# Converting float64 weights in a fused attention, SoLU and mixture-of-experts kernel: the magnitude pass rebiases the exponent, three VectorE steps instead of four

## The chip, the cores and the metric

One core of a Trainium2 chip runs the whole program. The metric is device time of one execution in microseconds; the kernel before has a median of 421.72 us over three runs (421.53 to 422.84). The profile is of one further execution that took 421.23 us, with a span of 419.5 us from its first to its last recorded instruction; the 1.73 us between the two lie outside the span.

## The reference

The program is three layers in a row, all in float32 apart from three inputs that arrive as float64:

```python
x = attn(q, k, v)                       # local band plus an attention pooled by 4; rows of 512
h = x @ w_in                            # (1152, 512) @ (512, 1024); w_in is float64
sm = softmax(h); solu = h * sm
ln = (solu - mu) / sqrt(var + 1e-6) * g_ln
x = (ln @ w_out).astype(float32)        # (1152, 1024) @ (1024, 512); w_out is float64
e = argmax(x @ w_gate); y = gate * relu(x @ w1[e]) @ w2[e]     # 8 experts, capacity from an input
```

`w_in` and `w_out` are random float32 values times a Python-side float64 factor, so their words are true float64 numbers of ordinary size (magnitudes of about 0.1 and less). The kernel turns each into a float32 and splits that into a high part and a low part for TensorE.

## The kernel before, in words

Work is tiled by 128 rows. There are nine row tiles, i = 0 to 8. For each tile, `loc_scores`, `loc_T` and `loc_AV` compute the local attention, `finish` (line 466) adds the pooled part to give `x32` (line 472) and splits it into `xh` (ScalarE, 478) and `xl` (VectorE, 479). `gemm1(i)` (491) is 24 TensorE matmuls of 128x512 into the two PSUM banks `gp`, three products (xh·wh, xl·wh, xh·wl) for each of four row blocks of `w_in`. `row(i)` (512) takes the row maximum `nm` on VectorE (515), the exponent on ScalarE (518), and one VectorE product (522), which is the last reader of `gp`: the first matmul of `gemm1(i+1)` waits for it. `gemm2(i)` follows a tile later, and after tile 8 come the experts, whose weights (32 chunks of 1 MB) stream in by DMA.

The conversion is `conv_steps(c)` (173), for eight pieces: c = 0 to 3 are the four row blocks of `w_in`, 4 to 7 the four pairs of row blocks of `w_out`. A piece is 128 x 1024 float64 numbers in one of three 1 MB buffers `rawb` (`conv_load`, 161). Below, "conv c" is piece c, `mag{c}` and `cv{c}` are its two tiles of 128x1024 words, and its operations are, by line of the kernel before:

- 185, ScalarE: `mag` is the absolute value of the high words, read as float32.
- 186, VectorE TENSOR_SCALAR: the high words shifted left by 3 and masked.
- 189, VectorE SCALAR_TENSOR_TENSOR: sign and top exponent bit of the high words or-ed in.
- 192, VectorE SCALAR_TENSOR_TENSOR: the low words shifted right by 29 and or-ed in. It is the last VectorE reader of `rawb`.
- 195, VectorE SCALAR_TENSOR_TENSOR, the guard: `cv` times (`mag` >= a threshold), which makes numbers below float32's range zero.
- 202, ScalarE, twice for conv 4 to 7: times `g_sb`; 208, ScalarE: the high part; 209, GpSimd (POOL): the low part, cv minus high part.

The tiles `mag` and `cv` come from one group of four buffers (tag t4), which they share with `he` and `sq` of `row`.

TensorE and SyncE keep the order in which the code stands (`manual_schedule`). VectorE, ScalarE and GpSimd are ordered when the program is built, by a scheduler with its own idea of durations; each then runs its instructions strictly in that order. `PLAN` (1056) says where the conversions stand in the code: conv 0 and 1 in the pooled attention, conv 2 to 4 ahead of tile 0, conv 5 beside `loc_scores(1)`, the first two steps of conv 7 in `gemm1(0)`, conv 6 and the rest of conv 7 after it. A load into `rawb` for conv c+3 is issued once 192 of conv c and its 185 are done.

Of the kernel before, what the change touches and what calls it, by code (L numbers as in the profile page):

```python
# [14 lines left out]
U32 = mybir.dt.uint32  # L15
AF = mybir.ActivationFunctionType
ALU = mybir.AluOpType
# [10 lines left out]
def kernel(  # L28
# [14 lines left out]
    nc = tc.nc  # L43
# [106 lines left out]
        nc.vector.tensor_scalar(cap_s, cap_f, float(CS), None, ALU.min)  # L150


    THR = float(np.uint32(897 << 20).view(np.float32))
    win_h, win_l, wout_h, wout_l = {}, {}, {}, {}
    raw64 = {}

# [16 lines left out]
    def conv_steps(c):  # L173

        raw = raw64.pop(c)
        n = 1024
        hl = raw.bitcast(U32).rearrange("p (n two) -> p n two", two=2)
        hi_w, lo_w = hl[:, :, 1], hl[:, :, 0]
        hf = raw.rearrange("p (n two) -> p n two", two=2)[:, :, 1]
        mag = bp.tile([P, n], F32, tag="t4", name=f"mag{c}", bufs=NT4)  # L180
        a = bp.tile([P, n], F32, tag="t4", name=f"cv{c}", bufs=NT4)
        au = a.bitcast(U32)

        def shift():
            nc.scalar.activation(mag, hf, AF.Abs)
            nc.vector.tensor_scalar(au, hi_w, 3, 0x3FFFFFFF, ALU.logical_shift_left, ALU.bitwise_and)

        def top():
            nc.vector.scalar_tensor_tensor(au, hi_w, 0xC0000000, au, ALU.bitwise_and, ALU.bitwise_or)

        def low():
            nc.vector.scalar_tensor_tensor(au, lo_w, 29, au, ALU.logical_shift_right, ALU.bitwise_or)

        def split():
            nc.vector.scalar_tensor_tensor(a, mag, THR, a, ALU.is_ge, ALU.mult)
            if c < KD:
                ch, cl, cc, nm = win_h, win_l, c, "in"
            else:
                ch, cl, cc, nm = wout_h, wout_l, c - KD, "out"
                for j in range(2):  # L200
                    aj = a[:, j * 512:(j + 1) * 512]
                    nc.scalar.activation(aj, aj, AF.Copy, scale=g_sb[:, 2 * cc + j:2 * cc + j + 1])
            g, o = divmod(cc, 2)
            if o == 0:
                ch[g] = ring.tile([P, 2048], F32R, tag="wh", name=f"w{nm}h{g}")
                cl[g] = ring.tile([P, 2048], F32R, tag="wl", name=f"w{nm}l{g}")
            sl = slice(o * n, (o + 1) * n)
            nc.scalar.activation(ch[g][:, sl], a, AF.Copy)
            nc.gpsimd.tensor_tensor(cl[g][:, sl], a, ch[g][:, sl].bitcast(F32), ALU.subtract)

        return [shift, top, low, split]

    def conv(c):
# [1117 lines left out]
```

## Time and profile before

| | |
|---|---|
| median of three runs | 421.72 us (421.53 to 422.84) |
| the profiled execution | 421.23 us, span 419.5 us |
| TensorE matmul (PE) busy | 355.6 us, 85% of the span |
| VectorE (DVE) busy | 202.3 us, 48% |
| ScalarE (ACT) busy | 167.8 us, 40% |
| GpSimd (POOL) busy | 120.2 us, 29% |
| mean granted clock of TensorE | 0.936 of full speed |

A timeline row of the profile reads: start, duration, engine, line, operation, out<-in, partitions x elements, count, and in brackets how long the engine was idle before and what ended that. A duration can contain waiting inside the instruction (for an SBUF port, say), which then does not show in brackets. The granted clock is 1.00 for 2.4 GHz and 0.50 for 1.2 GHz. Busy shares over the whole span say little here, since the program has stages with different limits: attention and conversion up to about 95 us, nine tiles of two matrix products up to about 245 us, the experts to the end.

### The profile page before, as it was taken

To read this page: it belongs to the slowest core of one execution; us is meant where nothing else is said; L and a number is where in the kernel's file an instruction comes from. 1 tells how busy PE (TensorE), PEld (TensorE's weight loads), DVE (VectorE), ACT (ScalarE), POOL (GpSimd) and SP (SyncE) were. 2 spreads that over 40 slices of the span, in tenths; PEclk is the share of its full clock that TensorE was granted. 3 is DMA by queue.
4 is the path that set the end of the run, shared out by engine and by line. 5 is a ranking of instruction groups with operands and counts; after the bars stand their busy time and mean duration, and the time that the engine had idled before them with its cause. 6 is when DMAs were issued, how large, how long until landed. Compare 5 with 4: busy or idle time off the path is not lost. (4 is left out here: it accounts for less than half of the span.)

```text
span 419.5 us, 7278 instructions
## 1 busy us (share of the span) xinstructions
PE 355.6 (85%) x2718; PEld 307.0 (73%) x2719; DVE 202.3 (48%) x486; ACT 167.8 (40%) x432; POOL 120.2 (29%) x170
## 2 busy tenths in 40 slices
PE   3546638299999999999999979679998999999991
PEld 3435526187767687777878769679988999999990
DVE  0685999866374979989445541102111111120210
ACT  3557537686686565565435312111120111111110
POOL 6693725479903020340220111001020202020111
PEclk9986558779999999999999999998999999999997
DMA  8998537233099345127196119999999740010001
GB/s 219 247 156 173 202 124 224 79 98 99 1 361 279 94 135 173 75 80 225 41 297 254 40 54 311 387 385 392 405 389 345 240 145 29 3 43 2 29 23 41
DMA packets 43783, 72.38 MB, mean 173 GB/s; under 512 B 15238, under 2 KB 17542, under 8 KB 42960
## 3 DMA queue, kind: packets, MB, share of 16 engines
q1 hardware_dynamic: 40080, 60.30, 46.3%
q0 software_dynamic: 3648, 11.30, 7.5%
q8 instruction: 39, 0.64, 0.6%
q14 instruction: 16, 0.13, 0.1%
HBM read 57.91 MB, written 15.52 MB: 175 GB/s over the span
## 5 line engine op out<-in xcount | busy, mean ns | idle before, releaser
L1016 POOL DMA_INDIRECT out_dram<-yo,js x16 | 15.6, 974 | 136.5 <-ACT yo L1013 113.2
L916 DVE TENSOR_SCALAR h<-ap 128x512 f32<-128x512 f32 x16 | 11.1, 692 | 71.0 <-PE ap L910 71.0
L500 PE MATMUL gp<-winh,xh 128*128 128x512 f32 x72 | 30.8, 428 | 13.3 <-DVE he L522 8.4
L918 ACT ACTIVATE h<-xp 128x512 f32<-128x512 f32 x16 | 9.6, 597 | 80.6 <-PE xp L910 80.6
L500 PE MATMUL gp<-winh,xl 128*128 128x512 f32 x72 | 31.6, 439 | 2.5 <-DVE xl L479 2.5
L500 PE MATMUL gp<-winl,xh 128*128 128x512 f32 x72 | 31.7, 440 | 0.0
L936 PE MATMUL yp<-h,wr 128*128 128x136 f32 x256 | 30.3, 279 | 0.0
L936 PEld LDWEIGHTS yp<-h,wr 128*128 128x128 f32 x256 | 30.0, 190 | 0.0
L607 DVE SCALAR_TENSOR_TENSOR prod<-x,rawb 128x512 f32<-128x512 f32 x40 | 28.3, 709 | 1.0 <-ACT x L568 0.6
L942 DVE COPY yT<-yp 128x512 f32<-128x512 f32 x7 | 4.8, 692 | 48.4 <-PE yp L936 42.0
L562 PE MATMUL xp<-wouth,lh 128*128 128x512 f32 x64 | 27.7, 433 | 0.0
L500 PEld LDWEIGHTS gp<-winh,xh 128*128 128x128 f32 x72 | 14.5, 202 | 16.1 <-issue 8.7
L562 PE MATMUL xp<-woutl,lh 128*128 128x512 f32 x64 | 26.2, 409 | 0.0
L670 POOL DMA_INDIRECT xd<-x,sloti x9 | 9.3, 1032 | 46.9 <-DVE efs L636 17.7
L415 ACT ACTIVATE e<-ls,lnm 128x70 f32<-128x70 f32 x68 | 20.6, 321 | 5.0 <-DVE lnm L412 4.9
L910 PE MATMUL xp<-xc,wr 128*128 128x136 f32 (+1 forms) x128 | 19.6, 307 | 1.6 <-DMA xg<-xd 1.6
L910 PEld LDWEIGHTS xp<-xc,wr 128*128 128x128 f32 x128 | 18.5, 196 | 1.8 <-issue 1.8
L500 PEld LDWEIGHTS gp<-winh,xl 128*128 128x128 f32 x72 | 14.4, 200 | 6.4 <-DVE xl L479 3.3
L910 PE MATMUL ap<-xc,wr 128*128 128x136 f32 (+1 forms) x128 | 19.0, 302 | 0.0
L936 PE MATMUL yp<-h,cpw 128*128 128x136 f32 (+1 forms) x128 | 19.0, 309 | 0.0
L936 PEld LDWEIGHTS yp<-h,cpw 128*128 128x128 f32 x128 | 18.7, 190 | 0.0
L562 PE MATMUL xp<-wouth,ll 128*128 128x512 f32 x64 | 18.6, 407 | 0.0
(262 smaller groups left out, 871.1 us busy)
## 6 DMA issues: line engine op xcount, KB each, us to landing
wr<-in_moe_w_dram SPq DMA_DIRECT2D x32, 512.0 KB
rawb<-in_moe_w_dram SPq DMA_DIRECT2D x16, 512.0 KB
cpw<-in_moe_w_dram SPq DMA_DIRECT2D x16, 512.0 KB
xd<-init POOLq DMA_DIRECT2D x2, 2056.0 KB, 17.4
xg<-xd SPq DMA_DIRECT2D x16, 257.0 KB
rawb<-in_moe_w_in_dram SPq DMA_DIRECT2D x8, 512.0 KB
rawb<-in_moe_w_out_dram SPq DMA_DIRECT2D x4, 1024.0 KB
xr<-x SPq DMA_DIRECT2D x9, 257.0 KB
```

What stands on the lines that cost most here:

```text
L415: nc.scalar.activation(e[:, a, pair], pv[:, pair], AF.Exp, bias=nm[:, u:u + 1], accum_out=sums[:, u:u + 1])
L500: nc.tensor.matmul(st["hp"][:, f * 512:(f + 1) * 512], xx[:, c * P:(c + 1) * P], ww[:, o * 1024 + f * 512:o * 1024 + (f + 1) * 512], start ...
L562: nc.tensor.matmul(st["ps"], xx[:, o * P:(o + 1) * P], ww[:, o * 512:(o + 1) * 512], start=(n == 0), stop=(n == 3 * KF - 1))
L607: nc.vector.scalar_tensor_tensor(prod, x2_t[i][:, :DM], 1.0, row, ALU.mult, ALU.mult, accum_out=st["lg"][:, e:e + 1])
L670: nc.gpsimd.indirect_dma_start(out=xd, out_offset=bass.IndirectOffsetOnAxis(ap=sloti, axis=0), in_=x2_t[i], in_offset=None, bounds_check=E ...
L910: nc.tensor.matmul(bank[:, j, :T], w[:, o:o + P], xc[:, c, :T], start=(c == 0), stop=(c == KD - 1))
L916: nc.vector.tensor_scalar(h, bank, 0.0, None, ALU.max)
L918: nc.scalar.activation(h, bank, AF.Relu)
L936: nc.tensor.matmul(bank[:, j, :T], w_t["w2", e, f // 4][:, o:o + P], h_t[e][f // 2][:, f % 2, :T], start=(f == 0), stop=(f == KF2 - 1))
L942: nc.vector.tensor_copy(yT, bank)
L1016: ins = nc.gpsimd.indirect_dma_start(out=out, out_offset=bass.IndirectOffsetOnAxis(ap=is_t[e][:, a:a + 1], axis=0), in_=yo_t.pop((e, a)), ...
```

## The change

[...] The first VectorE step takes the low words alone; the second shifts `mag` left by 3 and or-s it in; the third adds the sign bit. The guard (195) is gone. So there are three VectorE steps for each of eight conversions instead of four, and the second step now reads what ScalarE wrote, which the fourth did before.

```diff
-    THR = float(np.uint32(897 << 20).view(np.float32))
+    REBIAS = 2.0 ** -112
...
         def shift():
-            nc.scalar.activation(mag, hf, AF.Abs)
-            nc.vector.tensor_scalar(au, hi_w, 3, 0x3FFFFFFF, ALU.logical_shift_left, ALU.bitwise_and)
+            nc.scalar.activation(mag, hf, AF.Abs, scale=REBIAS)
+            nc.vector.tensor_scalar(au, lo_w, 29, None, ALU.logical_shift_right)
 
         def top():
-            nc.vector.scalar_tensor_tensor(au, hi_w, 0xC0000000, au, ALU.bitwise_and, ALU.bitwise_or)
+            nc.vector.scalar_tensor_tensor(au, mag.bitcast(U32), 3, au, ALU.logical_shift_left, ALU.bitwise_or)
 
         def low():
-            nc.vector.scalar_tensor_tensor(au, lo_w, 29, au, ALU.logical_shift_right, ALU.bitwise_or)
+            nc.vector.scalar_tensor_tensor(au, hi_w, 0x80000000, au, ALU.bitwise_and, ALU.bitwise_or)
 
         def split():
-            nc.vector.scalar_tensor_tensor(a, mag, THR, a, ALU.is_ge, ALU.mult)
             if c < KD:
```

The scheduler also puts the remaining instructions in another order. TensorE's order is the same in both. Lines from 195 on have a number lower by one in the changed kernel (472 becomes 471, 515 becomes 514). In the rows, a name ends with the piece or tile and a buffer number: `cv4_529` is conv 4's `cv`, `x32_0` is tile 0's.

VectorE, from conv 3 to the low part of tile 0's input, before:

```order
L186 TENSOR_SCALAR cv3_519<-rawb0_64 128x1024
L189 SCALAR_TENSOR_TENSOR cv3_519<-rawb0_64,cv3_519 128x1024
L192 SCALAR_TENSOR_TENSOR cv3_519<-rawb0_64,cv3_519 128x1024
L195 SCALAR_TENSOR_TENSOR cv3_519<-mag3_518,cv3_519 128x1024
L186 TENSOR_SCALAR cv4_529<-rawb1_65 128x1024
L189 SCALAR_TENSOR_TENSOR cv4_529<-rawb1_65,cv4_529 128x1024
L472 TENSOR_TENSOR x32_0_500<-ap_99,outd_115 128x512
L192 SCALAR_TENSOR_TENSOR cv4_529<-rawb1_65,cv4_529 128x1024
L412 TENSOR_REDUCE lnm1_557<-ls10_558 128x4
L479 TENSOR_TENSOR xl0_503<-x32_0_500,xh0_502 128x512
```

The same place in the changed kernel:

```order
L186 TENSOR_SCALAR cv3_516<-rawb0_64 128x1024
L189 SCALAR_TENSOR_TENSOR cv3_516<-mag3_515,cv3_516 128x1024
L192 SCALAR_TENSOR_TENSOR cv3_516<-rawb0_64,cv3_516 128x1024
L186 TENSOR_SCALAR cv4_525<-rawb1_65 128x1024
L189 SCALAR_TENSOR_TENSOR cv4_525<-mag4_524,cv4_525 128x1024
L192 SCALAR_TENSOR_TENSOR cv4_525<-rawb1_65,cv4_525 128x1024
L471 TENSOR_TENSOR x32_0_498<-ap_99,outd_115 128x512
L186 TENSOR_SCALAR cv5_587<-rawb2_66 128x1024
L411 TENSOR_REDUCE lnm1_552<-ls10_553 128x4
L189 SCALAR_TENSOR_TENSOR cv5_587<-mag5_586,cv5_587 128x1024
L411 TENSOR_REDUCE lnm1_552<-ls11_568 128x4
L478 TENSOR_TENSOR xl0_501<-x32_0_498,xh0_500 128x512
```

The guard of conv 3 is gone, the last step of conv 4 stands ahead of tile 0's `x32` where it stood behind it, and two steps of conv 5 with two row maxima stand between `x32` and `xl`.

VectorE, from the lsum of tile 1's local attention to the row maximum of tile 0, before:

```order
L418 TENSOR_SCALAR lsum1_556<-lsum1_556 128x8
L195 SCALAR_TENSOR_TENSOR cv5_592<-mag5_591,cv5_592 128x1024
L148 SCALAR_TENSOR_TENSOR cap_f_81<-capf2_549 128x1
L419 RECIPROCAL lsum1_556<-lsum1_556 128x8
L186 TENSOR_SCALAR cv7_642<-rawb1_65 128x1024
L150 TENSOR_SCALAR cap_s_82<-cap_f_81 128x1
L189 SCALAR_TENSOR_TENSOR cv7_642<-rawb1_65,cv7_642 128x1024
L192 SCALAR_TENSOR_TENSOR cv7_642<-rawb1_65,cv7_642 128x1024
L195 SCALAR_TENSOR_TENSOR cv7_642<-mag7_641,cv7_642 128x1024
L472 TENSOR_TENSOR x32_1_663<-ap_99,outd_115 128x512
L515 TENSOR_REDUCE nm0_671<-gp_108 128x1
```

The same place in the changed kernel:

```order
L417 TENSOR_SCALAR lsum1_551<-lsum1_551 128x8
L148 SCALAR_TENSOR_TENSOR cap_f_81<-capf2_544 128x1
L418 RECIPROCAL lsum1_551<-lsum1_551 128x8
L150 TENSOR_SCALAR cap_s_82<-cap_f_81 128x1
L189 SCALAR_TENSOR_TENSOR cv7_636<-mag7_635,cv7_636 128x1024
L192 SCALAR_TENSOR_TENSOR cv7_636<-rawb1_65,cv7_636 128x1024
L471 TENSOR_TENSOR x32_1_657<-ap_99,outd_115 128x512
L514 TENSOR_REDUCE nm0_665<-gp_108 128x1
```

Both guards are gone, and the first step of conv 7 stands further ahead: two steps of conv 7 are left between the lsum's reciprocal and `x32_1`.

ScalarE, from the high part of conv 5 to the exponent of tile 0, before:

```order
L208 ACTIVATE wouth0_537<-cv5_592 128x1024
L442 ACTIVATE eT10_630<-lt10_625 70x512
L442 ACTIVATE eT11_638<-lt11_633 70x512
L202 ACTIVATE cv7_642<-cv7_642,g_sb_78 128x512 x2
L478 ACTIVATE xh1_665<-x32_1_663 128x512
L208 ACTIVATE wouth1_697<-cv7_642 128x1024
L518 ACTIVATE he0_673,se0_674<-gp_108,nm0_671 128x1024
```

The same place in the changed kernel:

```order
L207 ACTIVATE wouth0_532<-cv5_587 128x1024
L201 ACTIVATE cv7_636<-cv7_636,g_sb_78 128x512 x2
L207 ACTIVATE wouth1_690<-cv7_636 128x1024
L441 ACTIVATE eT10_624<-lt10_619 70x512
L441 ACTIVATE eT11_632<-lt11_627 70x512
L477 ACTIVATE xh1_659<-x32_1_657 128x512
L517 ACTIVATE he0_667,se0_668<-gp_108,nm0_665 128x1024
```

The three passes for conv 7 stand ahead of the two copies `eT1` that tile 1's local attention needs on TensorE; they stood behind them, one of them just ahead of tile 0's exponent.

## Rows read from the trace of the kernel before

**Rows 1.** Stretches by engine: us, busy of PE, PEld, DVE, ACT, POOL; PEclk, DMA

```profile
59.00:83.00 24.00, 11.74 (x98) 8.38 (x98) 22.53 (x29) 15.03 (x45) 10.94 (x5) 0.78 0.48 143
...
95.00:240.00 145.00, 144.18 (x1119) 110.38 (x1118) 100.68 (x334) 84.95 (x243) 42.58 (x64) 1.00 0.48 156
...
262.00:323.00 61.00, 52.63 (x422) 51.67 (x421) 9.50 (x15) 8.32 (x14) 4.89 (x10) 0.97 1.05 389
```

**Rows 2.** TensorE's second longest wait after 83.1 us: us in total, times, longest

```profile
PE xp L910 <- issue: 3.0, 2, 1.6
```

**Rows 3.** TensorE's timeline from tile 0's first product to tile 1's

```profile
61.71 0.80 PE L500 MATMUL gp<-winh,xl 128*128 128x512 f32 x1 [2.19 <-DVE xl L479]
...
69.53 0.63 PE L438 MATMUL lt<-ident,e 128*70 128x128 f32 x4 [1.73 <-POOL e L421]
...
72.64 0.39 PE L500 MATMUL gp<-winl,xh 128*128 128x512 f32 x1
...
83.04 0.77 PE L500 MATMUL gp<-winh,xh 128*128 128x512 f32 x1 [8.38 <-DVE he L522]
```

**Rows 4.** VectorE's timeline, conv 2 to tile 0's xl

```profile
38.43 0.69 DVE L186 TENSOR_SCALAR cv<-rawb 128x1024 uint32<-128x1024 uint32 x1 [3.21 <-DMA rawb<-in_moe_w_in_dram]
...
46.81 2.73 DVE L186 TENSOR_SCALAR cv<-rawb 128x1024 uint32<-128x1024 uint32 x1
...
56.19 1.23 DVE L189 SCALAR_TENSOR_TENSOR cv<-rawb,cv 128x1024 uint32<-128x1024 uint32 x1
57.33 0.68 DVE L472 TENSOR_TENSOR x<-ap,outd 128x512 f32<-128x512 f32 x1
57.93 2.77 DVE L192 SCALAR_TENSOR_TENSOR cv<-rawb,cv 128x1024 uint32<-128x1024 uint32 x1
...
60.62 0.44 DVE L412 TENSOR_REDUCE lnm<-ls 128x4 f32<-128x280 f32 x1
60.98 0.68 DVE L479 TENSOR_TENSOR xl<-x,xh 128x512 fp32r<-128x512 f32 x1
```

**Rows 5.** VectorE's timeline, tile 1's lsum, conv 7's guard and tile 0's row

```profile
66.47 0.16 DVE L418 TENSOR_SCALAR lsum<-lsum 128x8 f32<-128x8 f32 x1
...
73.99 3.18 DVE L195 SCALAR_TENSOR_TENSOR cv<-mag,cv 128x1024 f32<-128x1024 f32 x1
...
77.69 1.21 DVE L515 TENSOR_REDUCE nm<-gp 128x1 f32<-128x1024 f32 x1
...
81.60 1.28 DVE L522 SCALAR_TENSOR_TENSOR he<-gp,se,he 128x1024 f32<-128x1024 f32 x1
```

**Rows 6.** GpSimd's timeline, conv 3's and conv 7's low part and tile 1's e

```profile
56.59 3.02 POOL L209 TENSOR_TENSOR winl<-cv,winh 128x1024 fp32r<-128x1024 f32 x1 [4.85 <-ACT winh L208]
68.11 1.37 POOL L421 TENSOR_TENSOR e<-e,lsum 128x560 f32<-128x560 f32 x1 [8.49 <-DVE lsum L419]
...
80.08 2.34 POOL L209 TENSOR_TENSOR woutl<-cv,wouth 128x1024 fp32r<-128x1024 f32 x1 [3.99 <-ACT wouth L208]
```

**Rows 7.** ScalarE's timeline around tile 0's row

```profile
70.20 1.26 ACT L442 ACTIVATE eT<-lt 70x512 f32<-70x512 f32 x2
77.20 1.33 ACT L202 ACTIVATE cv<-cv,g_sb 128x512 f32<-128x512 f32 x2 [5.74 <-DVE cv L195]
...
78.96 1.04 ACT L208 ACTIVATE wouth<-cv 128x1024 fp32r<-128x1024 f32 x1
79.91 1.09 ACT L518 ACTIVATE he<-gp,nm 128x1024 f32<-128x1024 f32 x1
```

**Rows 8.** TensorE alone in three stretches: us, busy; granted clock, DMA

```profile
83.00:89.00 6.00, 5.96 (x20) 0.50 0.14 39
```

**Rows 9.** All engines around a gap among the experts, as Rows 1

```profile
280.30:282.60 2.30, 0.00 (x0) 0.00 (x0) 0.00 (x0) 0.60 (x1) 0.00 (x0) 1.00 1.03 380
282.90:287.00 4.10, 4.10 (x24) 4.10 (x24) 0.69 (x1) 0.00 (x0) 0.00 (x0) 0.61 1.05 386
```

**Rows 10.** SyncE's timeline: the experts' first streamed chunks

```profile
254.43 16.73 SPq L707 DMA_DIRECT2D wr<-in_moe_w_dram  x16
```

## The prediction

> **What bounds the kernel now.** I read the table of stretches first. From 95 to 240 us TensorE is busy 144.2 of 145 us at a granted clock of 1.00 [rows 1]: nothing can be won there, but nothing is loose there either, so whatever starts earlier goes on earlier. From 59 to 83 us it is the other way round: TensorE is busy 11.7 of 24 us, VectorE 22.5 [rows 1]. So VectorE's queue bounds the program there, and that is where four of the eight conversions stand. Then TensorE's waits: after 83 us its longest is for 8.4 us [rows 3] and the next group sums to 3.0 us [rows 2]. The 8.4 us end with the first matmul of `gemm1(1)` at 83.04, which waits for VectorE's 522 of tile 0, the last reader of `gp` [rows 3].
>
> Why is 522 late? The last matmul of `gemm1(0)` starts at 72.64 and takes 0.39, so `gp` is whole at 73.03 [rows 3]. VectorE takes its row maximum `nm` only at 77.69, since the guard of conv 7 runs until 77.17 and `x32_1` follows it [rows 5]. Then `nm` is done at 78.90, but ScalarE's exponent starts at 79.91, because 208 of conv 7 stands ahead of it (78.96, 1.04 us) [rows 5, 7]. From the exponent's start to 83.04 it is 3.13 us.
>
> A second thing is to be seen in the durations. 192 of conv 4 takes 2.77 us at 57.93, where a three-operand step on 1024 words takes 1.23 [rows 4]; it ends at 60.70, one step after GpSimd's 209 of conv 3, which ends at 59.61 [rows 6]. 472 at 57.33 runs in the middle of that 209 and takes its usual 0.68 [rows 4, 6]. So the conversion steps, which read SBUF, do not run beside 209, while 472, which takes its products from PSUM, does; and each 209 (2.34 us alone [rows 6]) can cost the step that meets it up to that. The guard's 3.18 us at 73.99 and 186's 2.73 us at 46.81 are such cases, 186 alone taking 0.69 [rows 4, 5].
>
> **The change, part by part.** Eight guards of 1.2 us go, about 10 us of VectorE's time. The other three steps are of the same kind and size: one TENSOR_SCALAR (0.69), two SCALAR_TENSOR_TENSOR (1.23 each) [rows 4], and the scale in ScalarE's pass is an operand that the instruction has anyway; I count both at nothing. Where the trace has no such form (one operation in place of two, a contiguous operand in place of a strided one) the bounds are a step like 186, half as long, and one like 189: 0.5 us either way per step. What matters is the path, in four terms. I go from 38.43, where VectorE stops waiting for conv 2's data [rows 4]; that load was issued ahead of all this, so this point stays.
>
> *1. To `x32_0` (57.33).* From 38.43 on VectorE runs 13 conversion steps ahead of `x32_0`; now it is 11, since the guards of conv 1, 2 and 3 go and 192 of conv 4 comes in front of `x32_0`. That is 2 x 1.2 = 2.4 us less. But that 192 is the step that met 209 of conv 3, and its extra 1.55 us (2.77 less 1.22) now lie ahead of `x32_0`. Sum: 0.85 us earlier, at 56.5. Bounds: 2.4 earlier, if 209 is missed, and 0 with a whole 209 of 2.34.
>
> *2. From `x32_0` to `xl0`.* Before, 3.65 us (57.33 to 60.98) [rows 4]. Now 472 (0.6 from start to start), 186 of conv 5 (0.6), two row maxima (0.36 each from start to start) and 189 (1.2) stand there [rows 4]: 3.1 us, so `xl0` could start at 59.6. ScalarE, though, now has conv 4's two products by `g` (1.33), then `xh` (0.6, as `xl`), then 208 (1.04) [rows 4, 7] from 56.5 on, so 209 of conv 4 can start at about 59.5 and hold until 61.8. `xl0` reads SBUF alone, as the conversion steps do, so I take it that it waits: 61.8, and the first xl matmul, 0.73 us later as before (60.98 to 61.71), at 62.5 instead of 61.71: **0.8 us lost**. If `xl0` comes first, it is 60.3: 1.4 us won. This hangs on a tenth of a microsecond, so both ends are in the range.
>
> The Trainium skill's page SBUF — State Buffer (Who interferes with whom) says that the port pair of VectorE and GpSimd is an exclusive lock, taken by a VectorE instruction with two SBUF inputs or in a two-port mode, and that issue order decides who blocks. The trace agrees: 192 waited, 472, which reads PSUM, did not. By that rule alone `xl0`, with two SBUF inputs, waits out whatever is left of 209, 2.2 us as I took it; without it the sum would be 2.2 us better.
>
> *3. `gemm1(0)`.* Before, TensorE works for 6.1 us from 61.71, then waits 1.73 us for tile 1's `e` (421) until 69.53 [rows 3]; `e` waited for the lsum that stood behind guards [rows 5, 6]. Now it gets to that place at 68.6. After `xl0` (to 62.4) VectorE has 192 of conv 5 (to 63.6), 186 of conv 7 (64.2), six small ones of about 0.1 us, as 418 [rows 5], (64.8), and 189 of conv 7 (66.0); `e` follows within 1.4 us [rows 6], by 67.3, so this wait goes. 192 of conv 7 then ends at 68.5. ScalarE now does conv 7's products and high part (1.33 + 1.04) ahead of the copies `eT1` (1.26) [rows 7], so these end at 72.1 instead of 71.46. The last matmul ended 1.57 us after them (73.03), so `gp` is whole at 73.7: **0.6 us later than before**, the gain given back to the new order of ScalarE.
>
> *4. Tile 0's row.* Now nothing but `x32_1` (0.6) stands between the last products and `nm`: `nm` at about 73.8, done at 75.0, and nothing stands ahead of the exponent: 75.1 instead of 79.91. **4.8 us won**, and with 3.13 us as before `gemm1(1)` starts at 78.2 instead of 83.04.
>
> *5. The clock.* TensorE's idle time ahead of `gemm1(1)` shrinks from 8.4 to about 3 us. After the 8.4 us it works at clock 0.50, 1.2 GHz, from 83.0 to 89.0 [rows 8], which costs half, 3.0 us. After an idle stretch of 2.3 us among the experts it was at 0.61 on average over 4.1 us [rows 9], 1.6 us lost there, and some 2 with the edges. Between these I take 2.1 lost: **0.9 won**. Bounds: 0, as before, and 3.0, if it stays at 1.00.
>
> From there nothing else should move: TensorE has no gaps until 240 us, and the tiles' loads and stores follow its progress. Conv 6 loses its guard too, which nobody waits for. The experts' weights come at 389 GB/s with the DMA engines full from 262 to 323 us [rows 1], but their stream is issued from 254.43 on, behind the end of the last tile [rows 10], so it moves along. Sum: 4.8 + 0.9 = 5.7 us. Against the profiled execution, 421.23, that is 415.5. The median of the runs is 0.49 above it, so I predict 416.0.
>
> **The rivals.** A measurement here can tell about 0.3%, 1.3 us.
>
> *A. Luck with the port and the clock.* `xl0` gets ahead of 209, which brings the chain of term 3 forward by up to 2.2 us, and the clock keeps its level through the shorter gap (2.1 more): 416.0 less 4.3 is 411.7. For it: both hang on tenths of a microsecond. Against it: a gap of 2.3 us was enough to bring the clock down [rows 9], though the two that sum to 3.0 us [rows 2] left the stretch around them at 0.97 [rows 1].
>
> *B. The port takes the gain.* VectorE's remaining steps are closer together, so more of them can meet a 209. Each that conv 7's steps meet moves `eT1` by 2.34: one gives 418.3, two 420.7. For it: conv 7's guard met one in the trace [rows 5], and its steps now come sooner after 209 of conv 4. Against it: that one would have to be still running 5 us after its start, or conv 5's to start before 68.5.
>
> *C. ScalarE's new order makes it slower.* TensorE now waits for `eT1` behind conv 7's three ScalarE passes. The change is worth nothing from the point where `eT1` ends 4.8 us later than forecast, at 76.9, with the clock as low as before. With three 209 met (7.0 us) `gp` is whole at 80.7, and the clock's 0.9 goes: 415.5 + 7.0 + 0.9 is 423.4, and 423.9 as a median. Against it: only the 209 of conv 4 and of conv 5 are left for conv 7's steps to meet.
>
> *D. The gain is swallowed later.* Were the experts' stream not moved, TensorE, idle 8.4 us among them from 262 to 323 [rows 1], would wait that much more: 421.7. Against it: rows 10.
>
> **How the numbers follow.** The forecast, 414.0 to 418.0 with its own bounds (terms 1 and 5), has 0.6; A 0.12; B 0.15, most of it with one 209; C 0.05; D 0.08. The range reaches from 412.5, inside A, to 419.8, between B's two: outside lie the rest of A, the second step of B, C and D. Faster by over 0.3% (under 420.4): the forecast, A and most of B, 0.86. Within 0.3%: D and the end of B, 0.09. Slower: C, 0.05.
>
> **What would show it.** Right: the eight guards gone and nothing else longer; `nm` of tile 0 within 0.5 us of `x32_1`'s end and that right behind the last matmul's partners; the exponent right behind `nm`; TensorE's wait before `gemm1(1)` near 3 us in place of 8.4; the same order and length of everything after it. Wrong in a step: `x32_0` after 58, `xl0` before 60.5 or after 63, `eT1` ending after 74, a granted clock of 0.50 for 6 us after 78. Wrong as a whole: `gemm1(1)` earlier by 5 us and the end not.

## The result

| | before | after |
|---|---|---|
| median of four runs each, on one chip | 421.97 us (421.53 to 422.84) | 416.0 us (415.32 to 418.32) |
| the profiled execution, its span | 421.23 us, 419.5 us | 415.32 us, 413.6 us |
| VectorE busy | 202.3 us | 192.9 us |
| ratio to before, 95% interval | | 0.9866, 0.9824 to 0.9907 |

The kernel is 1.3% faster: 6 us, where 5.7 were predicted.

The scale 2**-112 in ScalarE's magnitude pass moves the exponent from float64's bias to float32's: the high word, read as float32, has the top eight of the eleven exponent bits, and 112 is (1023 - 127) / 8. What becomes of numbers below float32's range without the guard, no run here shows; there are none in this input.

VectorE's timeline in the kernel after, from conv 2's data to tile 0's row:

```profile
39.58 0.69 DVE L186 TENSOR_SCALAR cv<-rawb 128x1024 uint32<-128x1024 uint32 x1 [4.73 <-DMA rawb<-in_moe_w_in_dram]
...
47.68 3.26 DVE L192 SCALAR_TENSOR_TENSOR cv<-rawb,cv 128x1024 uint32<-128x1024 uint32 x1
50.86 2.84 DVE L186 TENSOR_SCALAR cv<-rawb 128x1024 uint32<-128x1024 uint32 x1
53.80 3.18 DVE L189 SCALAR_TENSOR_TENSOR cv<-mag,cv 128x1024 uint32<-128x1024 uint32 x1
...
58.16 0.68 DVE L471 TENSOR_TENSOR x<-ap,outd 128x512 f32<-128x512 f32 x1
...
61.22 2.84 DVE L478 TENSOR_TENSOR xl<-x,xh 128x512 fp32r<-128x512 f32 x1
...
73.70 0.69 DVE L471 TENSOR_TENSOR x<-ap,outd 128x512 f32<-128x512 f32 x1 [4.21 <-PE ap L458]
74.36 1.22 DVE L514 TENSOR_REDUCE nm<-gp 128x1 f32<-128x1024 f32 x1
```

These answer to [rows 4, 5]. No guard is left; `nm` stands directly behind `x32_1`, and VectorE, which was busy without a gap there, has waited 4.21 us for TensorE. Three steps in a row take about 3 us each (47.68 to 56.98), and `xl0` takes 2.84 in place of 0.68. GpSimd's timeline says why:

```profile
46.63 9.27 POOL L208 TENSOR_TENSOR winl<-cv,winh 128x1024 fp32r<-128x1024 f32 x3 [2.00 <-ACT winh L207]
61.16 2.34 POOL L208 TENSOR_TENSOR woutl<-cv,wouth 128x1024 fp32r<-128x1024 f32 x1 [5.26 <-ACT wouth L207]
```

The low parts of conv 1 to 3 now follow each other without a pause from 46.63 to 55.90, and each holds one step of VectorE; that of conv 4 starts 0.06 us before `xl0`. TensorE's timeline, for [rows 3], and then stretches of 1 us, for [rows 8] (columns as in [rows 1]; behind the busy times of the five engines stands the granted clock):

```profile
64.11 0.80 PE L499 MATMUL gp<-winh,xl 128*128 128x512 f32 x1 [3.12 <-DVE xl L478]
...
73.92 0.40 PE L499 MATMUL gp<-winl,xh 128*128 128x512 f32 x1
...
78.82 0.65 PE L499 MATMUL gp<-winh,xh 128*128 128x512 f32 x1 [2.86 <-DVE he L521]
```

```profile
79.00:80.00 1.00, 1.00 (x3) 0.81 (x3) 0.65 (x3) 1.00 (x3) 0.11 (x1) 0.50 0.00 0
...
81.00:82.00 1.00, 1.00 (x5) 0.77 (x4) 0.15 (x1) 1.00 (x3) 0.63 (x2) 0.50 0.07 16
82.00:83.00 1.00, 1.00 (x9) 0.85 (x7) 0.44 (x1) 1.00 (x3) 1.00 (x3) 0.82 0.00 0
```

The wait ahead of `gemm1(1)` is 2.86 us in place of 8.38, and TensorE works at a granted clock of 0.50 (1.2 GHz) for some 3.5 us after it, not 6.

**Where the time went.** One point that the prediction held fixed is not: conv 2's data landed at 38.43 before and at 39.58 now, and between 39.2 and 40.8 in the twelve traces that follow. SyncE issues that load at 22.04 before and at 22.99 now, but in the other traces (22.8 to 24.4) a later issue doesn't mean a later landing, and what moves it stays open. So times up to the end of `gemm1(1)` are counted from that landing in this document. The landing is the start of VectorE's step that waits for the DMA; `gp` is whole at the end of its last matmul; "rest" is the span less the end of `gemm1(1)`.

| us from the landing | landing | `x32_0` | first xl matmul | `gp` whole | `gemm1(1)` starts | ends | rest |
|---|---|---|---|---|---|---|---|
| before | 38.43 | 18.90 | 23.28 | 34.60 | 44.61 | 56.72 | 324.4 |
| after | 39.58 | 18.58 | 24.53 | 34.74 | 39.24 | 50.93 | 323.1 |

The span fell by 5.9 us: 1.15 were lost by the later landing, 5.37 won up to the start of `gemm1(1)`, 0.42 within it, and 1.26 in the rest.

### The profile page after: what moved, and what is told of

Same layout as the page of the kernel before. It is cut to its first block, busy times and chain, and to the rows that moved or that the text cites. A ratio compares the mean times of both kernels' runs of the same rounds, so it can differ in the third digit from the quotient of the medians.

```text
span 413.6 us, 7274 instructions
## 1 busy us (share of the span) xinstructions
PE 357.8 (86%) x2718; PEld 307.5 (74%) x2719; DVE 192.9 (47%) x478; ACT 167.6 (41%) x432; POOL 119.0 (29%) x170
## 5 line engine op out<-in xcount | busy, mean ns | idle before, releaser
L1015 POOL DMA_INDIRECT out_dram<-yo,js x16 | 15.6, 974 | 135.0 <-ACT yo L1012 111.7
```

What stands on the lines that cost most here:

```text
L1015: ins = nc.gpsimd.indirect_dma_start(out=out, out_offset=bass.IndirectOffsetOnAxis(ap=is_t[e][:, a:a + 1], axis=0), in_=yo_t.pop((e, a)), ...
```

## The experiments

All but one (the guard taken out of the kernel before) stand on the kernel after, and each has a profile; lines added by an edit shift the numbers behind them. Ratios are to the kernel before in runs of the same group; single runs of one kernel differ by 1% and more, so the fronts are read from the traces, in the measure above. Four of the traces ("fourth step, not 5, 7", "low part later", "warm early", "plan and warm") are of the longest run of their kernel, which bears on their column "rest":

| | landing | `x32_0` | first xl | `gp` whole | `gemm1(1)` | ends | rest | ratio, 95% interval |
|---|---|---|---|---|---|---|---|---|
| after again | 39.67 | 18.58 | 24.52 | 34.73 | 39.23 | 50.94 | 323.4 | 0.9857, 0.9806 to 0.9908 |
| fourth step, all | 39.23 | 17.85 | 23.97 | 35.43 | 45.09 | 56.28 | 323.9 | 1.0008, 0.9977 to 1.0038 |
| fourth step, conv 7 | 40.77 | 18.58 | 24.51 | 37.34 | 42.39 | 53.82 | 321.9 | 0.9922, 0.9889 to 0.9955 |
| fourth step, not 5, 7 | 40.52 | 17.85 | 23.97 | 38.36 | 43.45 | 55.21 | 325.4 | 0.9914, 0.9876 to 0.9952 |
| before, no guard | 39.46 | 20.84 | 25.47 | 36.63 | 41.13 | 53.73 | 324.0 | 0.9919, 0.9878 to 0.9959 |
| warm | 40.56 | 18.59 | 24.53 | 34.74 | 39.25 | 50.92 | 318.4 | 0.9789, 0.9745 to 0.9833 |
| warm again | 40.45 | 18.58 | 24.51 | 34.73 | 39.24 | 50.92 | 319.3 | 0.9777, 0.9734 to 0.9819 |
| warm early | 40.45 | 18.58 | 24.52 | 35.56 | 40.06 | 51.75 | 320.9 | 0.9801, 0.9759 to 0.9843 |
| low part later | 39.44 | 18.72 | 22.51 | 36.38 | 41.55 | 53.27 | 324.7 | 0.9891, 0.9843 to 0.9938 |
| both orders | 39.24 | 18.77 | 22.55 | 32.79 | 38.67 | 50.20 | 324.9 | 0.9829, 0.9784 to 0.9874 |
| plan | 39.77 | 12.84 | 16.50 | 28.75 | 33.11 | 48.70 | 321.5 | 0.9787, 0.9743 to 0.9832 |
| plan and warm | 39.99 | 14.80 | 17.44 | 31.81 | 36.95 | 53.14 | 321.6 | 0.9762, 0.9713 to 0.9811 |

### The kernel after, again

> The changed kernel itself once more, beside the others of this group on one chip, since the runs so far differ by over 1 us in when conv 2's data land (38.4 to 40.8 us), which none of the edits touches. Theory: counted from that landing, gemm1(1) starts 39.2 us later, within 0.5, as in the first trace of this kernel (before: 44.6), and the time is 5 to 6 us below that of the kernel before. Rival (part of the first result was a lucky run): more than 40.5 from the landing, or under 4 us below before.

No edit. All five points agree with the first trace to 0.02 us, from a landing 0.09 later. So the front was no lucky run. Two things besides an edit can still move these numbers: the scheduler may order anew, and a step can come just before or just behind a low part ("plan and warm" below).

### A fourth step put back

```diff
         def split():
+            nc.vector.scalar_tensor_tensor(a, mag, 0.0, a, ALU.is_ge, ALU.mult)
             if c < KD:
```

> The changed kernel with a fourth VectorE step put back into all eight conversions (cv times (mag >= 0), which is always one, so nothing else of the computation changes). Theory (the row maximum nm of tile 0 waits in VectorE's queue for the last step of conv 7): nm is again some 4 us behind the last matmul of gemm1(0), gemm1(1) starts near 83, and the median is 421 to 422.5, though the bits are made in the new way. Rival (the new operands and the scale in ScalarE's pass are what made the kernel faster, the step that went was covered): 416 to 417.

VectorE's timeline in this kernel, then TensorE's, the same way:

```profile
75.96 1.23 DVE L192 SCALAR_TENSOR_TENSOR cv<-rawb,cv 128x1024 uint32<-128x1024 uint32 x1
77.22 1.22 DVE L195 SCALAR_TENSOR_TENSOR cv<-mag,cv 128x1024 f32<-128x1024 f32 x1
78.37 0.68 DVE L472 TENSOR_TENSOR x<-ap,outd 128x512 f32<-128x512 f32 x1
78.97 1.21 DVE L515 TENSOR_REDUCE nm<-gp 128x1 f32<-128x1024 f32 x1
```

```profile
84.32 0.76 PE L500 MATMUL gp<-winh,xh 128*128 128x512 f32 x1 [6.99 <-DVE he L522]
```

The time is that of before, 421.43 us, though the bits are made in the new way. `gp` is whole at 74.66 and `nm` comes 4.3 us later, behind conv 7's last two steps. The rival falls: it is the step that went, not the form of the others. (`x32_0`, in another order, is even 0.7 us earlier than without the steps.)

The same line with `if c == 7:`

> The fourth step in conv 7 alone, one of eight. Theory: it is the step that stands last ahead of x32_1 and nm, and it meets GpSimd's low part of conv 5, so it takes 2 to 3.5 us in place of 1.2; gp is whole 1 to 2.5 us later and nm follows it at once, since here conv 7's products stand ahead of the copies eT1 on ScalarE. gemm1(1) near 81, median 417.5 to 419. Rival (the gain goes with the number of steps removed, 5.9 us for eight): 416.7, and nm not moved by more than 0.8 us.

VectorE's timeline, then GpSimd's:

```profile
70.70 3.30 DVE L195 SCALAR_TENSOR_TENSOR cv<-mag,cv 128x1024 f32<-128x1024 f32 x1
```

```profile
69.55 3.37 POOL L209 TENSOR_TENSOR woutl<-cv,wouth 128x1024 fp32r<-128x1024 f32 x1
```

The one step costs 3.15 us at the start of `gemm1(1)` (42.39 against 39.24), where an eighth of the gain would be 0.7. It takes 3.30 us, beside the low part of conv 5; ScalarE's products of conv 7 wait for it until 74.04, and the copies `eT1` stand behind them. `nm` follows `gp` at once, so here the step delays `gp`, not `nm`. `gp` moved by 2.60 us, a little over the range given; the other 0.55 lies between `gp` and `gemm1(1)` (5.05 us in place of 4.50).

And with `if c not in (5, 7):`

> The fourth step in six conversions, all but conv 5 and 7. Theory: no such step stands between the last products of conv 7 and nm, so nm follows the end of gemm1(0) within 0.5 us; what is lost is only that VectorE comes to conv 7's three steps later, by the one of conv 4 and what it meets (1.2 to 3.5 us), and with it eT1 and gp. gemm1(1) between 79.5 and 82.5, median 416.5 to 419.5. Rival (the number of steps): six eighths of the gain lost, 420.4, with gemm1(1) near 82.2 or later and nm behind gp.

`nm` starts 0.03 us behind the end of `gp`, as the theory has it, but `gemm1(1)`, at 43.45, is 4.2 us later than without the six steps. The end of the window, 82.5 with the landing of the kernel after, is 83.4 with this one; it is 83.97, a miss by 0.5. This number alone would fit the count of steps as well (six eighths of 5.37 are 4.0); the trial before and the place of `nm` speak against it. ScalarE's timeline shows where the time went, and VectorE's a part of it:

```profile
73.02 0.58 ACT L442 ACTIVATE eT<-lt 70x512 f32<-70x512 f32 x1
...
74.78 1.33 ACT L202 ACTIVATE cv<-cv,g_sb 128x512 f32<-128x512 f32 x2 [1.19 <-DVE cv L192]
76.02 0.58 ACT L442 ACTIVATE eT<-lt 70x512 f32<-70x512 f32 x1
```

```profile
71.28 2.33 DVE L148 SCALAR_TENSOR_TENSOR cap_f<-capf 128x1 f32<-128x1 f32 x1
```

The second copy `eT1` stands behind conv 7's products, which wait for VectorE's 192. So what stands ahead of conv 7 on VectorE is paid for over ScalarE's order. Some 2.2 of these us are no conversion step's own: ahead of that 192, a step of one column (0.15 us in the kernel before, 67.67) takes 2.33 beside a low part (GpSimd, from 70.87). The times decide nothing here. They spread most of all, from 414.03 to 422.76 us; the median of all twelve, 420.46, is the rival's number and lies outside the theory's window, while the ratio in the table, over the six shortest, lies inside it.

### The guard taken out of the kernel before

```diff
-            nc.vector.scalar_tensor_tensor(a, mag, THR, a, ALU.is_ge, ALU.mult)
```

> The kernel before with its guard taken out and nothing else: the old three steps, ScalarE's magnitude pass without a scale and now read by nobody (numbers below float32's range would not become zero; such numbers are not in this input). Theory: all of the gain comes from the queue, so 415.5 to 417, with nm within 0.5 us of the end of gemm1(0) and gemm1(1) between 78 and 80. Rival (the new form of the steps carries part of it): 418 or more.

`nm` is again right behind `gp` (76.13 and 76.09), and `gemm1(1)` 3.48 us earlier than before, two thirds of the 5.37. The other third is missing from `x32_0` on, which stands at 20.84 from the landing. VectorE's timeline:

```profile
58.44 0.69 DVE L186 TENSOR_SCALAR cv<-rawb 128x1024 uint32<-128x1024 uint32 x1
59.16 1.23 DVE L189 SCALAR_TENSOR_TENSOR cv<-rawb,cv 128x1024 uint32<-128x1024 uint32 x1
60.30 0.68 DVE L471 TENSOR_TENSOR x<-ap,outd 128x512 f32<-128x512 f32 x1
```

Two steps of conv 5 stand ahead of `x32_0`, which in the kernel after come behind it. They take 0.69 and 1.23 us, and 0.68 and 1.21 there. So the new form is no faster in itself; what comes with it is another order, in which 189 reads ScalarE's pass (that the scheduler orders otherwise for that reason was not tried). Both sides had something here: 418.73 us is the rival's number, and the part that came is the queue's.

### One low part later, and ScalarE's order

```diff
-            nc.gpsimd.tensor_tensor(cl[g][:, sl], a, ch[g][:, sl].bitcast(F32), ALU.subtract)
+            with ExitStack() as hold:
+                if c in (4,):
+                    t = tiny.tile([P, 1], F32, tag="tick", name=f"tick{c}", bufs=1)
+                    hold.enter_context(tc.issue_after(nc.gpsimd.tensor_copy(t, xl_t[0][:, 0:1].bitcast(F32)).ins))
+                nc.gpsimd.tensor_tensor(cl[g][:, sl], a, ch[g][:, sl].bitcast(F32), ALU.subtract)
```

> The changed kernel with one GpSimd step moved: the low part of conv 4 is held (by a GpSimd copy of one column of xl0) until xl0 is done. Theory (xl0's 2.84 us are 0.7 of its own and the rest this low part's hold on the port): xl0 takes 0.7 us and starts where it did, the first xl matmul is 2.1 us earlier counted from conv 2's landing (about 22.5 in place of 24.5 us). If that wait is on the path to gp, gemm1(1) is 1 to 2 us earlier too. Rival (the path runs through conv 7's steps, which wait for the buffer that this low part frees, and through e and eT1): gemm1(1) not earlier, or up to 1.5 us later.

VectorE's timeline and TensorE's:

```profile
61.21 0.68 DVE L482 TENSOR_TENSOR xl<-x,xh 128x512 fp32r<-128x512 f32 x1
...
63.39 2.60 DVE L186 TENSOR_SCALAR cv<-rawb 128x1024 uint32<-128x1024 uint32 x1 [0.36 <-DMA rawb<-in_moe_w_out_dram]
```

```profile
72.69 1.98 PE L462 MATMUL ap<-eT,vw 70*64 70x64 f32 x32 [2.25 <-ACT eT L445]
```

`xl0` starts within 0.13 us of where it did and takes 0.68: the 2.16 us more were the hold of the low part. The first xl matmul is 2.0 us earlier, and the front is slower all the same: `gp` 1.6 us later, `gemm1(1)` 2.3, more than the rival's 1.5. The low part, which now starts 2.0 us later (1.1 of that is the copy that holds it), holds 186 of conv 7 (2.60), and `eT1` comes 0.3 us later than it did. TensorE, ahead by 2 us, waits 2.25 us for it, and the granted clock behind that wait, from 72.7 to 75.8, is 0.50, where it was 1.00 in the kernel after: the products take 1.98 us in place of 1.17, and the two last matmuls are longer too. So the 2 us won at `xl0` became a wait for `eT1` and a slower clock. The times of the two kernels (417.06 and 415.8 us in one group) can't be told apart.

```diff
+        def split_late():
+            with tc.issue_after(eT_last[0]):
+                split()
...
-        return [shift, top, low, split]
+        return [shift, top, low, split_late if c == 7 else split]
...
-                nc.scalar.activation(eT, src, AF.Copy)
+                eT_last[0] = nc.scalar.activation(eT, src, AF.Copy).ins
```

> The changed kernel with two steps held back: GpSimd's low part of conv 4 until xl0 is done (as in the trial before), and ScalarE's products and high part of conv 7 until both copies eT1 are done. Theory (with the port's hold gone, it is conv 7's ScalarE passes ahead of eT1 that set gp): gp is whole 1.5 to 3.5 us earlier than in the changed kernel, at 31.3 to 33.2 us from the landing; of that up to 1.5 us are given back, since conv 7's high part then stands ahead of the exponent on ScalarE, as it did in the kernel before; gemm1(1) at 37.5 to 39 us. Rival (eT1 waits for e and the transposes anyway): gp within 0.5 us of 34.7 or later, gemm1(1) at 40 us or later.

With the same low part held and the copies `eT1` ahead of conv 7's passes, `gp` is whole at 32.79, 1.95 us earlier, as the theory has it. ScalarE's timeline, then VectorE's:

```profile
69.17 1.27 ACT L449 ACTIVATE eT<-lt 70x512 f32<-70x512 f32 x2 [2.48 <-PE lt L445]
70.34 1.33 ACT L201 ACTIVATE cv<-cv,g_sb 128x512 f32<-128x512 f32 x2
71.70 1.06 ACT L207 ACTIVATE wouth<-cv 128x1024 fp32r<-128x1024 f32 x1
```

```profile
73.56 2.17 DVE L486 TENSOR_TENSOR xl<-x,xh 128x512 fp32r<-128x512 f32 x1
```

Of that, 0.57 us are left at `gemm1(1)`: `xl1` now meets the low part of conv 7 (GpSimd, 72.83, 2.35 us) and takes 2.17 us, and the row's small steps stand behind it, at 76.01. ScalarE's order does set `gp`, and here most of what is won is lost again at the port.

### TensorE kept at work in its waits

```diff
                     mix(gemm2(i - 1) if i else [], *C)
+                    if i == 0:
+                        for _ in range(24):
+                            nc.tensor.matmul(yp[1][:, :CS], onesb, iota_s, start=True, stop=True)
```

> The changed kernel with 24 matmuls of constants (128x256, result read by nobody) on TensorE in its wait ahead of gemm1(1), 2.9 us long. Theory (the clock falls in that wait and costs 1.6 us after it): the granted clock stays at 1.00 from 75 to 90 us, gemm1(1) starts when it did, and its end comes 1.2 to 1.8 us earlier; median 1 to 2 us below the changed kernel. Rival (what follows in gemm1(1) waits for the transposes of tile 0's row and tile 2's e anyway): the clock stays up, and less than 0.5 us is left of it at the end of gemm1(1).

TensorE's timeline, and all engines in stretches (columns as in [rows 1]):

```profile
76.87 2.79 PE L1219 MATMUL yp<-iota_s,onesb 128*128 128x256 bf16 x24
79.81 0.47 PE L499 MATMUL gp<-winh,xh 128*128 128x512 f32 x1
...
89.20 0.52 PE L249 MATMUL tr_q<-ident,rows_q 128*128 128x128 f32 x3 [0.58 <-ACT kT L257]
```

```profile
80.00:82.00 2.00, 1.61 (x9) 1.02 (x8) 0.94 (x3) 1.97 (x4) 1.13 (x1) 1.00 0.00 0
...
84.00:91.00 7.00, 6.13 (x35) 4.52 (x35) 4.33 (x5) 5.46 (x11) 4.66 (x4) 1.00 0.49 147
```

The granted clock stays at 1.00 (2.4 GHz), `gemm1(1)` starts when it did, its first matmul takes 0.47 us in place of 0.65, and it ends at 50.92, when it did. What TensorE gains it spends waiting: inside `gemm1(1)` its waits sum to 1.25 us (0.39 for ScalarE's `he`, then 0.58 and 0.28 for its copies `kT`, ahead of the transposed rows of batch 1), where in the kernel after they are 0.18 and 0.29. So the clock after this wait is worth nothing here; the rival was right on the front. Yet the run is 3.5 us shorter than the kernel after in the same group (412.29 and 415.8 us); in the traces all of it is in the rest, 318.4 and 323.4.

> The trial with 24 matmuls of constants ahead of gemm1(1) once more. Theory (its 3.5 us among the experts were luck of that group of runs, since its front was no shorter): ratio to the kernel before 0.983 to 0.989, as the changed kernel. Rival (they belong to this program): 0.976 to 0.981 again, with gemm1(1)'s end at 50.9 us from the landing again.

The same kernel once more: the same front, and again a short rest, 319.3 us, and a ratio in the rival's window. So it comes with this program.

```diff
+                if i == 0:
+                    for _ in range(20):
+                        nc.tensor.matmul(yp[1][:, :CS], onesb, iota_s, start=True, stop=True)
                 mix(gemm1(i), *A)
```

> The changed kernel with 20 matmuls of constants in another wait of TensorE, the one of 5.2 us ahead of gemm1(0) (from 55 to 60 us). Theory (TensorE's clock is not on the path up to gemm1(1)): the first matmuls of gemm1(0) run at a higher granted clock, yet gp is whole 34.7 and gemm1(1) starts 39.2 us after conv 2's landing, as without them. For the rest it is a control of the trial with the matmuls ahead of gemm1(1): if adding some twenty instructions to TensorE's queue is what shortens the experts' stage, the ratio to the kernel before is 0.976 to 0.981 here too; if not, 0.984 to 0.989 as for the changed kernel.

One stretch of this kernel, then one of the kernel after (columns as above):

```profile
69.00:70.00 1.00, 1.00 (x4) 0.81 (x3) 1.00 (x1) 0.00 (x0) 1.00 (x2) 0.50 0.07 28
```

```profile
68.10:69.10 1.00, 1.00 (x5) 0.80 (x4) 1.00 (x1) 0.00 (x0) 1.00 (x2) 0.69 0.06 23
```

The theory falls: `gp` and `gemm1(1)` come 0.82 us later. The 20 matmuls end at 58.9 and the granted clock is 1.00 from 60 to 62; then TensorE waits 3.41 us for `xl0`, and from 65 to 70 it is at 0.50 again. In the kernel after, which idles before and between, it is back above 0.50 in the stretch shown, at 28.5 to 29.5 us from the landing; here not before 29.5. Here a higher clock ahead of another wait was a loss. As a control, the trial points to the added instructions: the rest is 320.9 us and the ratio 0.9801, in the window given for them, though its interval just reaches the other window.

### VectorE's queue once more: two entries of PLAN

In the third entry of PLAN 'a' becomes 'b', and the two entries of conv 7 become one. In PLAN, 'b' is behind `xl0` on VectorE, 'y' after `gemm1(0)`:

```diff
-    PLAN = ((2, 0, 4, 'a'), (3, 0, 4, 'a'), (4, 0, 4, 'a'), (5, 0, 4, 'm'), (6, 0, 4, 'y'), (7, 0, 2, 't'), (7, 2, 4, 'y'))
+    PLAN = ((2, 0, 4, 'a'), (3, 0, 4, 'a'), (4, 0, 4, 'b'), (5, 0, 4, 'm'), (6, 0, 4, 'y'), (7, 0, 4, 'y'))
```

> The changed kernel with two entries of PLAN changed: conv 4 stands behind xl0 on VectorE, and conv 7 wholly after gemm1(0). Theory (VectorE's queue is still what bounds the stretch up to gemm1(1)): x32_0 comes 3 to 4 us earlier, nothing of conv 7 stands ahead of eT1, gemm1(1) starts 4 to 6 us earlier; conv 6 and 7 then run beside gemm1(1), which takes 1 to 3 us longer, so 2 to 4 us of it are left at the end: median 412 to 414.5 if the kernel after is at 416. Rival (conv 6 and 7 come too late for gemm2(0)): gain at gemm1(1) and none or a loss at the end, 416 or more.

VectorE's timeline, then TensorE's:

```profile
52.61 0.69 DVE L471 TENSOR_TENSOR x<-ap,outd 128x512 f32<-128x512 f32 x1 [1.48 <-ACT outd L355]
```

```profile
72.88 0.47 PE L499 MATMUL gp<-winh,xh 128*128 128x512 f32 x1 [2.72 <-DVE he L521]
...
80.87 0.55 PE L249 MATMUL tr_k<-ident,rows_k 128*128 128x128 f32 x3 [2.28 <-POOL rows_k L244]
```

`x32_0` now waits for ScalarE, not in VectorE's queue, and is 5.7 us earlier; `gemm1(1)` starts 6.1 us earlier. It takes 15.6 us in place of 11.7: conv 6 and 7 run beside it, and GpSimd's `rows_k` come late (2.28 us of TensorE's wait). So 2.2 us are left at its end; the rest was 1.9 us shorter as well. At 411.87 us this is 0.9% faster than the kernel after in the same group. The front moved by more than the windows given, and the median came out just below its own.

> The two entries of PLAN moved (conv 4 behind xl0, conv 7 wholly after gemm1(0)) and the 24 matmuls of constants in the wait ahead of gemm1(1), together, in the changed kernel. In the two trials apart the clock stayed up but gemm1(1) did not end earlier, counted from conv 2's landing (50.9 us both), while the run was 3.5 us shorter, all of it among the experts. Theory (the matmuls of constants are worth nothing up to gemm1(1)'s end, and the experts' stage is 318 to 325 us long by how the weights happen to come in): gemm1(1) ends 48 to 49 us after the landing, as with PLAN alone, and the median is that of PLAN alone within 1.5 us, ratio to the kernel before 0.976 to 0.982. Rival (the two gains add up): 0.970 to 0.973.

The front is not that of PLAN alone: `gemm1(1)` ends 4.4 us later, and the window was missed. The order on VectorE is the same up to there. GpSimd's timeline and VectorE's in this kernel:

```profile
46.48 5.75 POOL L208 TENSOR_TENSOR winl<-cv,winh 128x1024 fp32r<-128x1024 f32 x2 [1.44 <-ACT winh L207]
```

```profile
46.83 3.18 DVE L189 SCALAR_TENSOR_TENSOR cv<-mag,cv 128x1024 uint32<-128x1024 uint32 x1
```

The low part of conv 1 starts 0.35 us before 189 of conv 3, which then takes 3.18 us. With PLAN alone 189 started at 46.61 and took 1.23, and the low part came after it, at 46.77. So a few tenths between two engines cost 2 us at `x32_0` in this run, the longest of its six (416.39 us; the others take 408.58 to 413.24). Whether the others met the same is not shown. The ratio, 0.9762, which leaves this run out, is not to be told from those of the two apart. All three beat the kernel before; the two apart also beat the kernel after in their group, by 3.9 and 3.5 us.

### The rest: what the added matmuls changed

TensorE among the experts, in the kernel after and in "warm again":

```profile
264.10 1.09 PE L871 MATMUL gg<-ident,xg 128*128 128x128 f32 x8 [1.57 <-issue]
...
276.80 3.78 PE L909 MATMUL ap<-xc,cpw 128*128 128x136 f32 x16 [2.34 <-issue]
```

```profile
267.92 3.97 PE L935 MATMUL yp<-h,cpw 128*128 128x136 f32 x32 [0.90 <-issue]
...
273.91 2.11 PE L909 MATMUL ap<-xc,cpw 128*128 128x136 f32 x16 [0.17 <-issue]
...
279.75 0.66 PE L1003 MATMUL y<-ident,yT 128*128 128x128 f32 x4 [1.44 <-issue]
```

The waits stand at other instructions and are shorter. "Issue" means that nothing the profile shows was waited for. Here a shorter wait counted twice: the sixteen matmuls at 276.80, behind 2.34 us, take 3.78 us at a granted clock of 0.55, and the same sixteen in "warm again", behind 0.17 us, 2.11 us at 1.00. Two rows of the DMA view of the kernel after, one for 261.0 to 261.5 us and one for 274.0 to 274.5 (queue, packets, MB, share of the 16 engines):

```profile
q8 instruction: 1, 0.02, 13.1%
```

```profile
q8 instruction: 1, 0.02, 13.7%
```

While the weights come in with all DMA engines full, packets of that queue come one at a time, 5.5 to 7 us apart, and the two waits end 2.3 to 3.1 us after one; in "warm again" the two end 2.2 to 2.9 us after the packets in 265.0 to 265.5 and 277.0 to 277.5. Around the start of that stream its packets are at 247, 251 and 259, those of the kernel after at 249, 255.5 and 261. That TensorE waits there for its own instructions, and that the added ones shift where a packet ends, would fit all of this. It is not shown: the view doesn't say whose instructions a packet holds, and no run changed that alone.

## Why the prediction was right

*The time*, 416.0 us, was met, by a main term that held and by errors that cancelled; that it was met to the tenth is luck. The change needs no rival: A (411.7), B (418.3 and more), C and D lie outside the interval, B only just, though B's mechanism acted on `xl0` and C's on `eT1`. That a measurement tells 0.3% was too much: the 29 runs of the kernel before that stand beside the first four trials reach from 418.55 to 425.66 us, and it is the traces that decide.

*Term 4*, the row, carries the gain. From `gp` whole to `gemm1(1)` it was to be 4.5 us in place of 10.0, and it is 4.50 in place of 10.01. With the fourth step back it is 9.66, with the guard out of the old kernel 4.50. The mechanism is shown. Of these 5.5 us, 4.8 were to be left at `gemm1(1)`; from the landing 5.37 are, and 4.22 by the trace's own clock.

*The steps that remain* were counted at nothing, and that holds: 189, where nothing on GpSimd holds it, takes 1.20 to 1.23 us in both kernels, and ScalarE's pass with its scale 1.14 us, against 1.15.

*Term 1*: 0.85 us earlier predicted, 0.32 measured from the landing. Ahead of `x32_0` low parts hold three steps now, where they held two; the sum had this third hold at 1.55 us, and the last of the three cost 1.95 (3.18 less 1.23). That conv 2's data land when they did was wrong by 1.15 us, and so `x32_0`, at 58.16, came behind the 58 that was named as a sign of a wrong step. Whether the change has a part in the landing stays open (the kernel with four new steps shows 39.23, the one trace of before 38.43).

*Term 2*: the first xl matmul was to come 0.8 us later and came 1.25 later; the 0.45 more is what term 1 lacked, since from `x32_0` to it 5.95 us were measured and 6.0 predicted. The prediction named the mechanism rightly: `xl0` takes 2.84 us, and 0.68 with the low part moved. The Trainium skill's page SBUF — State Buffer (Who interferes with whom) calls the port pair that VectorE and GpSimd share an exclusive lock, and both numbers agree with it. What the hold was worth was wrong: the prediction put the sum 2.2 us better without it, and in the run that moved it to another step `gemm1(1)` came 2.3 us later.

*Term 3*: `gp` 0.6 us later predicted, 0.14 measured, from a first xl matmul that was 1.25 late: the stretch between was 10.21 us, not 11.2. That `gp` hangs on `eT1` behind conv 7's passes is shown by "both orders".

*Term 5* is the step that failed. The clock came back sooner, as said (half of 3.5 us lost in place of half of 6), but the end of `gemm1(1)` moved by 0.42 us more than its start, not 0.9, and with the clock kept whole it did not move further (50.92 and 50.93). The prediction took TensorE to be without gaps from `gemm1(1)` on; inside `gemm1(1)` it now waits for other engines' work. The 1.26 us of the rest, which the prediction had at nothing, and the 1.15 us of the landing made up for each other.

## To carry to other kernels

Removing work from a busy engine is worth what stands in its queue ahead of the next wait on the path: one of eight like steps cost 3.15 us, where a mean share would be 0.7. Before a hold or a slow clock is priced, look who waits next behind it: here neither the hold on `xl0` nor the clock behind the wait gave back its price when it was taken away. And count the front from an event close ahead of it: a single landing moved by more than most terms (38.4 to 40.8 us).

## What was not expected

Some twenty matmuls more, read by nobody, went with a shorter stage some 160 us later: the rest is 318.4, 319.3 and 320.9 us with them and 323.1 and 323.4 in the two traces of the kernel after. With PLAN they made no difference, 321.6 and 321.5, and the ten traces without them reach from 321.5 to 325.4. TensorE's waits there are for something that the profile's releasers don't name. And the same step of VectorE took 1.23 us where it started 0.16 us before a low part, and 3.18 us where it started 0.35 us behind one's start.
